# The last unit's outputs stored by quadrants instead of by whole rows

## The chip, the cores and the metric

The kernel runs on one core of a Trainium2 chip. The time is the device time of one execution in microseconds. Before the change, seven runs gave a median of 497.47 us, from 496.6 to 498.04.

## What is computed

A linear attention over 8 batches of 8 heads (576 positions, 64 features per head) feeds a mixture of 4 expert MLPs whose outputs are added with normalised weights:

```python
q_p, k_p = phi(q), phi(k)                       # elu + 1
kv = einsum('bhsd,bhse->bhde', k_p, v)
x = (q_p @ kv) / (q_p . sum(k_p))               # 4608 tokens x 512
p = probs / (probs.sum(-1) + 1e-9)
for e in range(4):
    h = maximum(x @ w1[e], 0)                   # 512 -> 1024
    out += p[:, e:e+1] * (h @ w2[e])            # 1024 -> 512
```

The output is 4608 x 512 in float32, 9.4 MB.

## The kernel before

**Tiles and units.** The 4608 tokens are cut into nine tiles of 512 tokens: tile j below 8 holds the first 512 positions of batch j; tile 8 holds the last 64 positions of all eight batches. One tile with one expert is a unit, and the units run tile by tile, the four experts within each; the last unit is (8, 3). A tile's output is four blocks of 128 tokens by 512 columns, `accs[j, ns]`, each an SBUF tile of 128 partitions with one row of 2 KB per token. In tile 8, block `ns` has the tokens of batch `2 * ns` in partitions 0 to 63 and of batch `2 * ns + 1` in 64 to 127.

**Layer 2 by seven products.** From tile 1 on, each 2 x 2 product of half matrices is done as seven products instead of eight (a Strassen scheme; the scheme's sums are made on VectorE and GpSimd). `layer2_product(j, e, ..., p, i)` does product `p` for token sub-block `i` (0 or 1): four matmuls of 128 x 256 into a PSUM tile, and then `add_acc` (L562), which scales it by the expert's weight and adds it to one *quadrant*: block `ns` and columns `ds`, either the left half `c1` or the right half `c2`. A table at L677 says which: product 2 and 1 go to the left half of block `i`, 6 and 3 to its right half, 5 and 7 to the right half of block `2 + i`, and 4 to its left half. The adds run on VectorE (L570). In the last unit the order of the products is 1, 2, 6, 5, 7, 3, 4 (L965), each for `i` = 0 and then 1, and two pairs of PSUM buffers, `pb` and `pe`, take turns.

**The stores.** After product 3 or 4 of expert 3 the block is complete, and `store` (L548) writes it out. For tiles 0 to 7 that is one DMA from the SP queue, 128 rows of 2 KB (L551). For tile 8 it is two DMAs, one for each half of the partitions, since those are two batches (L557): `u = 0` goes from SP's queue and, in the last tile, `u = 1` from ACT's. So the kernel ends with eight stores of 128 KB each: for `i` = 0 and 1 after product 3, and for `i` = 0 and 1 after product 4.

**Order.** The order of all the work is written out by hand: each step has a position (`put_at`), the list is sorted by position and issued in that order, and each engine keeps its own order. Which instruction waits for which is derived by the framework from the parts of tiles that they read and write. Each DMA from SP or ACT tells of its landing on one of eight semaphores, which are taken in turn. At the very end (L1020) the program waits until all DMAs have landed and then runs through a short barrier of all the engines.

Of the kernel before, what the change touches and what calls it, by code (L numbers as in the profile page):

```python
# [80 lines left out]
def kernel(  # L81
# [10 lines left out]
    nc = tc.nc  # L92
    ATTN, HSUM, L2ORD, L2AT, MODE = (CFG[x] for x in ("ATTN", "HSUM", "L2ORD", "L2AT", "MODE"))

    B, H, S, D = q.shape
    N, E = moe_domain_probs.shape
    _, Dm, F = moe_w1.shape
# [4 lines left out]
    SM = CM * P  # L102
# [7 lines left out]
    NTILES = N // NT  # L110
# [62 lines left out]
    out_b = out.rearrange("(b s) d -> b s d", s=S)  # L173
# [341 lines left out]
    accs = {}  # L515
# [29 lines left out]
    def new_py():  # L545
        return ppm.tile([P, Dm], FP32, tag="py", bufs=2, name="py")

    def store(j, ns, last=False):  # L548
        acc = accs[j, ns]
        if j < B:  # L550
            nc.sync.dma_start(  # L551
                out=out_b[j, 0:SM].rearrange("(p c) d -> c p d", c=CM)[ns],
                in_=acc,
            )
        else:
            for u in range(2):
                (nc.scalar if last and u else nc.sync).dma_start(  # L557
                    out=out_b[2 * ns + u, SM:S],
                    in_=acc[u * HP : (u + 1) * HP],
                )  # L560

    def add_acc(j, e, ns, ps, ds, first):  # L562
        if (j, ns) not in accs:
            accs[j, ns] = pm.tile([P, Dm], FP32, tag="acc", bufs=NACC, name="acc")
        acc = accs[j, ns][:, ds]
        pscal = p_sb[:, j, ns, e : e + 1]
        if first:
            nc.scalar.activation(acc, ps, AF.Identity, scale=pscal)
        else:
            nc.vector.scalar_tensor_tensor(  # L570
                out=acc, in0=ps, scalar=pscal, in1=acc, op0=AO.mult, op1=AO.add
            )

    def layer2_part(j, e, ns, hT, part, parts):
        if part == 0:
            pys[ns] = new_py()
        py = pys[ns]
        for fj in range(part * FC // parts, (part + 1) * FC // parts):
            nc.tensor.matmul(  # L579
                out=py,  # L580
                lhsT=rows(hT, fj)[:, ns * P : (ns + 1) * P],
                rhs=w2_sb[e][:, fj, :],
                start=(fj == 0),
                stop=(fj == FC - 1),
            )
        if part == parts - 1:
            add_acc(j, e, ns, py, slice(0, Dm), e == 0)
            if e == E - 1:
                store(j, ns)
# [53 lines left out]
    def layer2_product(j, e, hT, hss, p, i):  # L643


        if (j, e) == (NTILES - 1, E - 1):
            if p == 1:
                pys[i] = [ppm.tile([P, DH], FP32, tag=tag, bufs=2, name=f"p{tag}") for tag in ("b", "e")]
            run, side = pys[i]
        else:  # L650
            if p == 2:
                pys[i] = new_py()
            run, side = pys[i][:, 0:DH], pys[i][:, DH:Dm]
        ts = slice(i * P, (i + 1) * P)
        ts2 = slice(NH + i * P, NH + (i + 1) * P)
        w, tw = w2_sb[e], t2_sb[e]
        lo, hi = slice(0, FH), slice(FH, FC)
        ps, lhsT, rhs, first = {
            1: (run, lambda k: hT[k // 2][:, k % 2, 0, ts], w[:, lo, 0:DH], (j, e) == (NTILES - 1, E - 1)),
            2: (side, lambda k: hT[k // 2][:, k % 2, 1, ts], w[:, hi, 0:DH], True),  # L660
            5: (side, lambda k: hss[k // 2][0][:, k % 2, ts], tw[:, 0], True),
            6: (run, lambda k: hss[k // 2][1][:, k % 2, ts], tw[:, 1], False),
            7: (run, lambda k: hT[k // 2][:, k % 2, 0, ts2], w[:, lo, DH:Dm], False),
            3: (side, lambda k: hss[k // 2][3][:, k % 2, ts], w[:, hi, DH:Dm], False),
            4: (run, lambda k: hT[k // 2][:, k % 2, 1, ts2], tw[:, 2], False),
        }[p]
        for k in range(FH):
            nc.tensor.matmul(  # L668
                out=ps,
                lhsT=lhsT(k),  # L670
                rhs=rhs[:, k],
                start=first and k == 0,
                stop=k == FH - 1,
                skip_group_check=True,
            )
        c1, c2 = slice(0, DH), slice(DH, Dm)
        ns, ds, first = {  # L677
            2: (i, c1, True),
            5: (2 + i, c2, True),
            1: (i, c1, False),  # L680
            6: (i, c2, True),
            7: (2 + i, c2, False),
            3: (i, c2, False),
            4: (2 + i, c1, True),
        }[p]
        add_acc(j, e, ns, ps, ds, first and e == 0)
        if e == E - 1 and p in (3, 4):
            store(j, ns, j == NTILES - 1)

    tts = {}  # L690

# [171 lines left out]
    with tc.manual_schedule(  # L863
# [87 lines left out]
        for n, (j, e) in enumerate(units):  # L951
            h, hss = [None, None], [[None] * 4, [None] * 4]
            at = base + 2 * NSLOT * n
            for d in range(2):
                put_block(at + d * NSLOT, j, e, d, h)
            at += 2 * NSLOT + LAG

            def hsum(d, i, hT=h, hss=hss):
                hidden_sum(hT[d], hss[d], i)

            for d in range(2):
                for i in range(4):
                    put_at(at + HSUM[d][i], hsum, d, i)
            order = L2ORD
            if n == len(units) - 1:  # L965
                order, at = (1, 2, 6, 5, 7, 3, 4), at + NSLOT
            for m in range(14):
                put_at(at + L2AT[m], layer2_product, j, e, h, hss, order[m // 2], m % 2)
# [56 lines left out]
```

## Time and profile before

| What | Before |
|---|---|
| Median of 7 runs | 497.47 us (496.6 to 498.04) |
| The profiled execution's own time | 497.47 us |
| Its span, first to last instruction | 495.2 us |
| TensorE clock granted | 0.999 of full |
| Sub-block adds on L570, one add of 128 x 256 | 0.48 us, starting 0.44 us apart in the last unit |
| Stores of tiles 0 to 7 (L551): 256 KB, SP, to landing | 2.5 us (median of 32) |
| Stores of tile 8 on SP (L557): 128 KB, to landing | 2.7 us (median of 4) |
| Stores of tile 8 on ACT (L557): 128 KB, to landing | 3.3 us (median of 4) |

The profile is one execution. It lists, for each engine, what ran when and what it waited for. TensorE appears as PE (the products) and PEld (the loading of weights), VectorE as DVE, ScalarE as ACT, GpSimd as POOL and SyncE as SP; a "q" behind the name means the engine's instruction queue, where DMAs are issued and semaphores are waited for. A DMA has two durations: how long its issue occupies the queue (the duration in the timeline), and how long it is from the start of the issue until the data has landed.

### The profile page before, as it was taken

How to read it: one execution, taken by the hardware profiler on the slowest of the kernel's cores; microseconds unless marked ns; L12 is line 12 of the kernel's file. 1: busy time of each engine (PE TensorE's matmuls, PEld its weight loads, DVE VectorE, ACT ScalarE, POOL GpSimd, SP SyncE). 2: the span in 40 equal slices, each digit the busy share in tenths (PEclk: the TensorE clock that was granted, in tenths of full speed). 3: DMA queues.
4: the chain of work that ended last, by engine and by line, in shares of the span. 5: the costliest groups of instructions: out<-in, count | busy, mean ns of one | idle time of the engine just before them, and what ended most of it. 6: DMA issues, size and time to landing. Idle time of an engine off the chain costs nothing.

```text
span 495.2 us, 11600 instructions
## 1 busy us (share of the span) xinstructions
PE 483.5 (98%) x4346; PEld 409.5 (83%) x4346; DVE 378.7 (76%) x802; ACT 336.5 (68%) x678; POOL 354.7 (72%) x339
## 2 busy tenths in 40 slices
PE   8999989999999999999999999999999999999995
PEld 3556656888898989898989898989898888888884
DVE  5757888798867887698859886888687756775685
ACT  5776969964987498848884789468954565446530
POOL 3735204778967897769776977697769877987773
PEclk9999999999999999999999999999999999999999
DMA  8999965552455245533463245523141020002002
GB/s 258 211 220 240 272 137 161 175 117 52 112 175 129 54 109 171 126 64 96 144 155 78 76 145 139 101 63 104 68 79 28 5 95 1 1 3 85 1 1 86
DMA packets 81561, 53.65 MB, mean 108 GB/s; under 512 B 46113, under 2 KB 74785, under 8 KB 81505
## 3 DMA queue, kind: packets, MB, share of 16 engines
q1 hardware_dynamic: 70272, 40.07, 30.9%
q0 software_dynamic: 9824, 11.27, 12.1%
q10 hardware_dynamic: 1408, 1.57, 1.0%
q8 instruction: 34, 0.56, 0.5%
q14 instruction: 23, 0.18, 0.1%
HBM read 45.16 MB, written 9.44 MB: 110 GB/s over the span
## 4 chain that ended last, share of the span: by engine, by line
PE 82%; DMA 10%; DVE 3%; POOL 1%; ACT 1%; issue 1%; ACTq 0%; DVEq 0%; POOLq 0%
PE py L668 38%; PE pb L730 22%; PE pe L730 16%; DMA w<-in_moe_w_dram 7%; DMA rawu<-in_q_dram 2%; PE py L579 2%; PE psum_nd L465 1%; DMA rawh<-in_k_dram 1%; PE psum_kv L425 1%; DVE acc L570 1%; DVE x_sb L448 1%; PE pb L668 1%; DVE h L714 0%; PE psum_nl L482 0%; PE pe L668 0%
## 5 line engine op out<-in xcount | busy, mean ns | idle before, releaser
L570 DVE SCALAR_TENSOR_TENSOR acc<-py,p_sb,acc 128x256 f32<-128x256 f32 (+1 forms) x382 | 182.3, 488 | 49.3 <-PE py L668 40.1
L714 DVE CUSTOM_DVE_ANT_0 h<-pe,u 128x512 f16<-128x512 f32 x140 | 96.3, 688 | 41.8 <-PE pe L730 26.8
L730 PEld LDWEIGHTS <-w 128*128 128x128 f16 x1120 | 108.8, 98 | 17.0 <-issue 1.4
L635 POOL TENSOR_TENSOR hs<-h 128x512 f16<-128x512 f16 x64 | 74.0, 1156 | 54.9 <-DVE h L714 53.6
L668 PEld LDWEIGHTS <-h 128*128 128x128 f16 x1024 | 99.6, 98 | 11.8 <-issue 0.5
L668 PE MATMUL py<-w,h 128*128 128x256 f16 x744 | 106.4, 273 | 0.0
L741 ACT COPY u<-pb 128x512 f32<-128x512 f32 x140 | 82.8, 591 | 27.5 <-PE pb L730 25.1
L637 POOL TENSOR_TENSOR hs<-hs,h 128x512 f16<-128x512 f16 x64 | 74.7, 1168 | 26.7 <-PE py L668 24.1
L730 PEld LDWEIGHTS <-s 128*128 128x128 f16 x840 | 81.6, 98 | 11.8 <-DVE s L607 0.4
L730 PE MATMUL pb<-tt,w 128*128 128x256 f16 x560 | 84.0, 273 | 0.7 <-ACT u L741 0.7
L668 PEld LDWEIGHTS <-hs 128*128 128x128 f16 x768 | 74.4, 98 | 9.9 <-issue 1.3
L641 POOL TENSOR_TENSOR hs<-h,hs 128x512 f16<-128x512 f16 x64 | 74.7, 1166 | 3.5 <-PE py L668 3.1
L668 PE MATMUL py<-t,hs 128*128 128x256 f16 x496 | 74.4, 272 | 0.6 <-DVE acc L570 0.4
L639 POOL TENSOR_TENSOR h<-h 128x512 f16<-128x512 f16 x64 | 74.5, 1165 | 0.0
L756 ACT ACTIVATE h<-pe 128x512 f16<-128x512 f32 x70 | 41.9, 598 | 44.9 <-PE pe L730 44.4
L750 ACT COPY pe<-pb 128x512 f32<-128x512 f32 x70 | 40.3, 575 | 41.5 <-PE pb L730 14.9
L774 ACT ACTIVATE h<-pb 128x512 f16<-128x512 f32 x70 | 41.9, 599 | 9.8 <-PE pb L730 9.7
L730 PE MATMUL pb<-tt,s 128*128 128x256 f16 x280 | 42.0, 273 | 0.1
L730 PE MATMUL pe<-tt,s 128*128 128x256 f16 x280 | 42.0, 273 | 0.0
L730 PE MATMUL pb<-xT,w 128*128 128x256 f16 x248 | 37.2, 273 | 0.2
L730 PE MATMUL pe<-xT,s 128*128 128x256 f16 x248 | 37.2, 273 | 0.1
L668 PE MATMUL py<-w,hs 128*128 128x256 f16 x248 | 37.2, 273 | 0.0
(120 smaller groups left out, 605.7 us busy)
## 6 DMA issues: line engine op xcount, KB each, us to landing
out_dram<-acc SPq DMA_DIRECT2D x32, 256.0 KB, 2.5
w<-in_moe_w_dram POOLq DMA_DIRECT2D x14, 512.0 KB, 13.0
rawb<-in_v_dram SPq DMA_DIRECT2D x26, 256.0 KB, 2.8
rawb<-in_q_dram SPq DMA_DIRECT2D x26, 256.0 KB, 2.8
rawb<-in_k_dram SPq DMA_DIRECT2D x26, 256.0 KB, 3.2
w<-in_moe_w_dram POOLq DMA_DIRECT2D x4, 256.0 KB, 5.8
rawb<-in_k_dram POOLq DMA_DIRECT2D x4, 256.0 KB, 11.4
rl<-in_q_dram SPq DMA_DIRECT2D x16, 64.0 KB, 2.6
```

Source lines behind the costliest of these rows:

```text
L570: nc.vector.scalar_tensor_tensor(out=acc, in0=ps, scalar=pscal, in1=acc, op0=AO.mult, op1=AO.add)
L635: nc.gpsimd.tensor_tensor(out=hs[0], in0=a21, in1=a22, op=AO.add)
L637: nc.gpsimd.tensor_tensor(out=hs[1], in0=hs[0], in1=a11, op=AO.subtract)
L639: nc.gpsimd.tensor_tensor(out=a21, in0=a11, in1=a21, op=AO.subtract)
L641: nc.gpsimd.tensor_tensor(out=hs[3], in0=a12, in1=hs[1], op=AO.subtract)
L668: nc.tensor.matmul(out=ps, lhsT=lhsT(k), rhs=rhs[:, k], start=first and k == 0, stop=k == FH - 1, skip_group_check=True,)
L714: nc.vector._custom_dve(TENSOR_ADD_SAT, out=out, in0=ps, in1=u, s0=BIG, s1=0.0)
L730: nc.tensor.matmul(out=ps[:, kk], lhsT=lk(kc), rhs=rhs[:, kc], start=first and kk == 0 and kc == 0, stop=kc == 1, skip_group_check=True,)
L741: nc.scalar.copy(u, self.b)
L750: nc.scalar.copy(self.e5, self.b)
L756: nc.scalar.activation(self.h[:, :, 0, 0:NH], self.e5, AF.Relu)
L774: nc.scalar.activation(self.h[:, :, 1, 0:NH], self.b, AF.Relu)
```

## The change

For the last unit alone, a store is made as soon as a quadrant is complete instead of a block: after products 2, 7, 3 and 4, for both values of `i`, `store` is called with the columns `ds` of that product. Each such store is 64 partitions by 256 columns, rows of 1 KB to every second KB of the output: 64 KB, once from SP and once from ACT. For all other units the calls are as before. The argument `last` goes, since the branch with two DMAs serves tile 8 only.

```diff
-    def store(j, ns, last=False):
-        acc = accs[j, ns]
+    def store(j, ns, cols=slice(0, Dm)):
+        acc = accs[j, ns][:, cols]
         if j < B:
             nc.sync.dma_start(
                 out=out_b[j, 0:SM].rearrange("(p c) d -> c p d", c=CM)[ns],
...
             for u in range(2):
-                (nc.scalar if last and u else nc.sync).dma_start(
-                    out=out_b[2 * ns + u, SM:S],
+                (nc.scalar if u else nc.sync).dma_start(
+                    out=out_b[2 * ns + u, SM:S, cols],
                     in_=acc[u * HP : (u + 1) * HP],
                 )
...
         add_acc(j, e, ns, ps, ds, first and e == 0)
-        if e == E - 1 and p in (3, 4):
-            store(j, ns, j == NTILES - 1)
+        if (j, e) == (NTILES - 1, E - 1):
+            if p in (2, 3, 4, 7):
+                store(j, ns, ds)
+        elif e == E - 1 and p in (3, 4):
+            store(j, ns)
```

## The prediction

> **What bounds the kernel, and where the change acts.** I read the engine shares first, then the last microseconds as a timeline, then the stretches after the last product.
>
> ```profile
> PE 483.5 (98%) x4346; PEld 409.5 (83%) x4346; DVE 378.7 (76%) x802; ACT 336.5 (68%) x678; POOL 354.7 (72%) x339
> ```
>
> TensorE bounds the body, and the diff touches no product, so only what follows the last products can move. The timeline's columns are start, duration, engine and line:
>
> ```profile
> 484.65 0.92 DVE L570 SCALAR_TENSOR_TENSOR acc<-pe,p_sb,acc 128x256 f32<-128x256 f32 x2
> ...
> 487.27 0.92 DVE L570 SCALAR_TENSOR_TENSOR acc<-pb,p_sb,acc 128x256 f32<-128x256 f32 x2
> ...
> 488.14 0.92 DVE L570 SCALAR_TENSOR_TENSOR acc<-pe,p_sb,acc 128x256 f32<-128x256 f32 x2
> ...
> 488.66 2.48 SPq L557 DMA_DIRECT2D out_dram<-acc  x4
> 488.66 2.77 ACTq L557 DMA_DIRECT2D out_dram<-acc  x4
> 489.02 0.92 DVE L570 SCALAR_TENSOR_TENSOR acc<-pb,p_sb,acc 128x256 f32<-128x256 f32 x2
> ```
>
> These pairs of adds are products 2, 7, 3 and 4 of the last unit. The last add ends at 489.94, yet the span ends at 495.2: 5.2 us in which no engine computes. The view of stretches (PE, PEld, DVE, ACT, POOL busy; clock; DMA share; GB/s) says what fills them:
>
> ```profile
> 490.00:491.00 1.00, 0.00 (x0) 0.00 (x0) 0.00 (x0) 0.00 (x0) 0.00 (x0) 1.00 0.99 279
> 491.00:492.00 1.00, 0.00 (x0) 0.00 (x0) 0.00 (x0) 0.00 (x0) 0.00 (x0) 1.00 0.88 295
> 492.00:493.00 1.00, 0.00 (x0) 0.00 (x0) 0.00 (x0) 0.00 (x0) 0.00 (x0) 1.00 0.92 305
> 493.00:494.00 1.00, 0.00 (x0) 0.00 (x0) 0.00 (x0) 0.00 (x0) 0.00 (x0) 1.00 0.37 137
> ```
>
> The eight 128 KB stores, 1.05 MB, keep the DMA engines 90% busy: a burst at some 300 GB/s. Read singly, the landings are:
>
> SP issues 488.66, 489.30, 489.94, 490.58; landings 491.05, 491.73, 492.91, 493.89.
> ACT issues 488.66, 489.33, 490.17, 490.83; landings 491.39, 492.72, 493.54, 494.07.
>
> The first land after 2.39 (SP) and 2.73 us (ACT), the last after 3.31 and 3.24. From 494.07, the kernel's exit takes 1.10 us to the span's end at 495.17. So **the end is set by the landing of the last ACT store**. The profiled execution took 497.47 us, 2.3 more than its span, and is equal to the median; I sum against it.
>
> The last issues are themselves late: their add ends at 489.94, they start at 490.58 and 490.83. The rows of the two queues say why (min/median/max ns):
>
> ```profile
> L557 SPq DMA_DIRECT2D out_dram<-acc x4: 547/551/552, 488.7 to 490.6; - x4
> L557 ACTq DMA_DIRECT2D out_dram<-acc x4: 571/612/802, 488.7 to 490.8; - x4
> ```
>
> An issue occupies its queue for 0.55 to 0.61 us, from start to next start 0.64 on SP (1.92 / 3) and 0.72 on ACT (2.17 / 3), while adds come every 0.44.
>
> **Part 1: twice the stores, half the size.** Eight stores of 128 KB become sixteen of 64 KB: 64 partitions by 1 KB. In the order 1, 2, 6, 5, 7, 3, 4 the last product of each quadrant is indeed 2, 7, 3 or 4, so the change does what it says. Nothing is removed but bytes per store. Four pairs move ahead: those after product 2 (ready 485.13, 485.57) and after product 7 (ready 487.75, 488.19). SP and ACT have nothing else queued (ACT's last activation ends at 480.27), so nobody waits behind them except the later stores. That is the price: each queue gets six issues from 487.75 on, where it had four from 488.63.
>
> What does such an issue cost? No store of this form is in the trace. Two rows are near:
>
> ```profile
> L551 SPq DMA_DIRECT2D out_dram<-acc x32: 332/357/604, 80.7 to 448.7; - x32
> ...
> L253 SPq DMA_DIRECT2D rl<-in_q_dram x16: 597/614/639, 65.4 to 379.8; - x16
> ```
>
> The first is a store of 128 partitions with a strided destination, the second a 64 KB transfer over 64 partitions. Both 64-partition forms, L557 and L253, are the dear ones, so I take L557's pitch, 0.64 and 0.72, and keep 0.42 (0.33 + 0.09) and 0.84 (0.80 + 0.04) as ends.
>
> Starting at 487.78 (0.03 after the add, as at 488.66), with A and B for product 2's two stores on a queue, C and D for product 7's, G and H for product 4's:
> SP: C 487.78, D 488.42, then 489.06, 489.70, 490.34, H 490.98.
> ACT: C 487.78, D 488.50, then 489.22, 489.94, 490.66, H 491.38.
> So **H goes out 0.40 (SP) and 0.55 us (ACT) later than today**.
>
> **Part 2: the landing after H.** Per DMA engine, one store is four packets; 2 KB packets of this burst took 84 ns, 1 KB packets of the loads 46. A halved store saves 4 x 38 ns = 0.15 us; an ACT store behind its SP twin saves that twice. Unloaded landings become 2.39 - 0.15 = 2.24 and 2.73 - 0.30 = 2.43. They stay unloaded if the DMA engines keep up: a pair is 8 x 46 = 0.37 us of packets in each 0.64 to 0.72. Then SP's H lands at 493.22, ACT's at 491.38 + 2.43 = **493.81, 0.26 us before 494.07**. The burst's queueing goes (some 0.8 us of landing), and most of it is given back in issue time.
>
> [...]
>
> **Part 3: a new wait on the store's semaphore.** Loads and stores from SP and ACT rotate over eight semaphores, and an issue waits until its predecessor on the same one has landed. The start of the kernel shows it: the ninth transfer goes out at 3.72 when the first ACT load landed at 3.70, others at 4.85 for 4.83 and 6.43 for 6.41.
>
> ```profile
> 3.72 1.04 SPq L275 DMA_DIRECT2D rawb<-in_v_dram  x2
> 4.85 0.42 SPq L275 DMA_DIRECT2D rawb<-in_q_dram  x1
> 6.43 0.37 SPq L275 DMA_DIRECT2D rawb<-in_k_dram  x1
> ```
>
> Eight stores in the tail used each semaphore once; sixteen use it twice: product 3's stores wait for product 2's (long landed), G for C, H for D. D lands at 488.42 + 2.24 = 490.66 (SP) and 488.50 + 2.43 = 490.93 (ACT), 0.32 and 0.45 us before H's turn: hidden by the queue. If D's landing takes over 2.9 us, H waits.
>
> **Part 4: a wait of the adds on a store?** Product 6 adds to the right half of a block whose left half is being read by a store. If the whole tile were guarded, its add would wait. The nearest case is x_sb: the transpose issued at 365.91 reads one part and lands at 368.39, and VectorE writes another part at 367.00:
>
> ```profile
> 365.91 1.19 SPq L509 DMA_TRANSPOSE xT<-x_sb  x1
> ...
> 367.00 0.56 DVE L448 TENSOR_TENSOR x_sb<-psum_nd,recip 128x384 f16<-128x384 f32 x1
> ```
>
> So parts are guarded apart, and I cost this at nothing. The `last` argument's removal costs nothing: the else branch only serves the last tile.
>
> **Sum.** -0.26 us: 497.47 - 0.26 = **497.2**. With the ACT pitch at its usual 0.67 it is -0.5; with 0.84, +0.34.
>
> **The rivals.**
> 1. *Issue is cheap.* If a strided half row issues at 0.42, H is no longer queue-bound (487.78 + 2.10 = 489.88) but held by D: issued 488.22, landed on ACT 490.65. H lands at 493.08: -0.99, **496.5**; with landings nearer to the 2.07 of L551's quiet stores, 496. For: L551's 0.33 with a strided destination. Against: both 64-partition rows.
> 2. *Slower: the DMA side charges by the transfer, not the byte.* The burst served eight stores from first packet 489.86 to last 493.64: 0.47 each. If that is per transfer, twelve from 488.98 (C's issue + 1.20) end at 494.62, plus 0.43 to land: 495.05, +1.0, **498.5**, with H also held by a late D. It decides from 0.39 us per transfer, (494.07 - 0.43 - 488.98) / 12. For: the very first store's packets took 161 ns, not 84, and ACT's began only 0.61 us after them. Against: the next ones began 0.33 to 0.36 apart, which is the byte price 4 x 84.
> 3. *The adds wait for stores.* Product 6's add waits from 485.52 to A's landing, 485.16 + 2.43 = 487.59: +2.07. Then product 4's (491.09) waits for C's (487.78 + 2.07 + 2.43 = 492.28): +1.19. With the gain, +3.0: **500.5**. Only x_sb speaks against it, plainly.
>
> **How the numbers follow.** A measurement here tells no change from about 0.2%, 1.0 us: faster is below 496.5, slower above 498.5. The forecast gets 0.56 (its own range 496.6 to 498.0, from the pitches; 0.04 faster, 0.48 same, 0.04 slower); rival 1 gets 0.20 (0.15 faster, 0.05 same); rival 2 gets 0.19 (0.15 slower, 0.04 same); rival 3 with anything unforeseen 0.05, slower. Sums: 0.19, 0.57, 0.24. The range runs from rival 1 to just past rival 2, leaving out the tails of 1, 2 and 3: 496.3 to 498.7.
>
> **What would show it.** Right: issues on L557 still 0.55 to 0.6 us, back to back from 487.8; H starting near 491.0 and 491.4, landing after some 2.3; the stretch 490 to 493 at a DMA share near half. Wrong: issues of 0.35, H starting at D's landing, ACT landings over 3 us, or an idle gap on VectorE ahead of products 6 or 4.

## The result and the profile after

The changed kernel takes **496.07 us** (median of 15 runs, 495.25 to 497.33) against 497.45 before (35 runs): ratio 0.9973, 95% interval 0.9966 to 0.9980, or 1.0 to 1.7 us less. The forecast was 497.2, with no change as the likeliest case and a range from 496.3: too slow, and the measured time lies 0.23 us below the range. Two later series gave 0.9979 (0.9973 to 0.9986) and 0.9975 (0.9966 to 0.9983).

The rows of the store line in the changed kernel (count, min/median/max ns of an issue, first and last start):

```profile
L557 SPq DMA_DIRECT2D out_dram<-acc x8: 467/547/553, 484.3 to 490.0; - x8
L557 ACTq DMA_DIRECT2D out_dram<-acc x8: 498/557/856, 484.3 to 490.3; - x8
...
DMA to landing us min/median/max: 1.9/2.0/3.7
```

An issue costs what it did, 0.55 us, though its store is half as large; a landing takes 2.0 us where the last ones took 3.3. The stretches after the last add, which ends at 489.05 here (PE, PEld, DVE, ACT, POOL busy; clock; DMA share; GB/s):

```profile
488.00:489.00 1.00, 0.53 (x5) 0.22 (x3) 1.00 (x3) 0.00 (x0) 0.00 (x0) 1.00 0.85 196
489.00:490.00 1.00, 0.00 (x0) 0.00 (x0) 0.05 (x1) 0.00 (x0) 0.00 (x0) 1.00 0.89 204
490.00:491.00 1.00, 0.00 (x0) 0.00 (x0) 0.00 (x0) 0.00 (x0) 0.00 (x0) 1.00 0.88 203
491.00:492.00 1.00, 0.00 (x0) 0.00 (x0) 0.00 (x0) 0.00 (x0) 0.00 (x0) 1.00 0.82 185
492.00:493.50 1.50, 0.00 (x0) 0.00 (x0) 0.00 (x0) 0.00 (x0) 0.00 (x0) 0.95 0.02 5
```

The burst of 300 GB/s has become an even stream of 200, and it ends before 492, not after 493. The DMA engines are still 82 to 89% busy: the packets have become slower for their size, of which more below.

Two numbers of each profile carry the study: the **tail**, from the end of the last add to the last landing, and the **exit**, from there to the end of the span. Issue and landing of the last stores, counted from the last add's end:

| | SP's last issue, landing | ACT's last issue, landing | Tail | Exit |
|---|---|---|---|---|
| Before, first profile | +0.65, +3.96 | +0.89, +4.14 | 4.14 | 1.10 |
| Forecast | +1.04, +3.28 | +1.44, +3.87 | 3.87 | 1.10 |
| After | +0.97, +3.01 | +1.29, +3.32 | 3.32 | 1.09 |

The spans of this first pair differ by 1.71 us, but only 0.82 of that is tail. The last add itself comes 0.89 earlier, and all of that is won in the first 160 us (0.86 of it by 70), where the two kernels have the same instructions. It is the spread of single executions, and the experiments have to part it from the change.

### The profile page after: what moved, and what is told of

Its sections match the earlier page's. It is cut to its first block, busy times and chain, and to the rows that moved or that the text cites. A ratio compares the mean times of both kernels' runs of the same rounds, so it can differ in the third digit from the quotient of the medians.

```text
span 493.5 us, 11616 instructions
## 1 busy us (share of the span) xinstructions
PE 482.6 (98%) x4346; PEld 409.2 (83%) x4346; DVE 378.4 (77%) x802; ACT 336.4 (68%) x678; POOL 354.6 (72%) x339
## 4 chain that ended last, share of the span: by engine, by line
PE 84%; ACT 7%; DVE 4%; DMA 2%; issue 1%; POOL 1%; ACTq 0%; DVEq 0%; POOLq 0%
PE py L668 38%; PE pb L733 22%; PE pe L733 16%; PE py L579 2%; PE ph L524 1%; PE psum_nd L465 1%; DVE x_sb L448 1%; ACT psum_ee L315 1%; ACT u L744 1%; DMA rawh<-in_k_dram 1%; DVE acc L570 1%; PE psum_kv L425 1%; DMA rawb<-in_v_dram 1%; ACT h L759 1%; ACT vp L332 1%
## 5 line engine op out<-in xcount | busy, mean ns | idle before, releaser
L733 PE MATMUL pe<-xT,w 128*128 128x256 f16 x248 | 37.2, 272 | 0.0
```

The lines of the kernel that those rows point to most:

```text
L733: nc.tensor.matmul(out=ps[:, kk], lhsT=lk(kc), rhs=rhs[:, kc], start=first and kk == 0 and kc == 0, stop=kc == 1, skip_group_check=True,)
```

## The experiments

**Twice more the changed kernel, once more the one before.** No edit.

> The changed kernel once more, to part what is lasting from what varies. In the first pair of profiles the last add to the last landing took 4.13 us before and 3.32 after (0.81 less), while the last add itself came 0.89 us earlier, all of it gained in the first 64 us, where no instruction differs. Theory 'tail': only the 0.81 are the change's; the median comes out 0.7 to 1.0 below the kernel before and the tail again at 3.3. Theory 'more than the tail': the median is again 1.3 to 1.5 below, and the last add or the time outside the span is again earlier by some 0.5.

> The changed kernel a third time, beside the former on the same chip: 0.8 to 1.1 us faster than the kernel before, tail 3.3, and the last landing 1.1 before the end of the span.

> The kernel before once more, with a profile. In the first profile of it the execution's own time was 2.30 us more than its span, in all eight others so far 1.77 to 1.87, so 0.5 us of the change's gain lie outside the span. Theory 'lasting': again 2.3 outside the span, and a tail of 4.1. Theory 'spread of one execution': 1.8 outside. The time itself: no change against the kernel before.

The three profiles of the changed kernel have tails of 3.32, 3.30 and 3.30 us; the two of the kernel before 4.14 and 4.25. The last add came at 489.05, 489.78 and 490.18 after, at 489.94 and 490.15 before. The tail's gain of 0.9 us is thus lasting. The series: 0.9979 and 0.9975 for the changed kernel as above, 1.0002 (0.9995 to 1.0010) for the kernel before. In the first profile of before, the execution's time was 2.3 us over its span, here 1.84. All the series together say more than these two: of 170 executions of the kernel before, 36 took 2.2 to 2.4 us outside their span and the others 1.9 at most; of 152 of the changed kernel and its variants, none took more than 2.04. On average the kernel before thus loses 0.1 to 0.2 us there against the changed one. What causes it stays open.

**Instructions alone.** Does the changed kernel gain from the mere number of instructions on the queues?

```diff
+        if (j, e, p) == (NTILES - 1, E - 1, 2):
+            for m in range(4):
+                (nc.scalar if m % 2 else nc.sync).dma_start(
+                    out=extra[:, i, m : m + 1], in_=moe_domain_probs[m * P : (m + 1) * P, 0:1]
+                )
```

> The kernel before, with eight tiny loads (one float per partition, never read) added ahead of the last stores, four on SP's and four on ACT's queue: as many instructions more as the change brings, all landed long before the tail. Theory 'the time outside the span hangs on the count of instructions on a queue': 1.8 outside the span as in the changed kernel, the tail still 4.1, and 0.5 us faster than the kernel before. Theory 'it hangs on the stores' (or on nothing): 2.3 outside, no change in the time.

Ratio 1.0005 (0.9997 to 1.0014), tail 4.29, 1.78 us outside the span. None of its 13 executions took over 1.9 us there, but the 0.5 us of gain that the theory forecast lies outside the interval: instructions alone don't make the changed kernel's time.

**Half size, but not early.**

```diff
-            if p in (2, 3, 4, 7):
-                store(j, ns, ds)
+            if p in (3, 4):
+                store(j, ns, c1)
+                store(j, ns, c2)
```

> Both halves of a block are stored, but only when the block is complete (after products 3 and 4): stores of half the size, none of them early. Theory 'the queue': eight issues each on SP and ACT, 0.64 us apart, from 1.28 us before the last add's end; the last starts 3.2 after it and lands 2.05 later: tail 5.2 to 5.3, 1.1 us slower than the kernel before. Theory 'size': shorter stores land sooner and that was the gain: tail 3.3 to 3.9. Theory 'bytes left': as many bytes after the last products as before, so tail 4.1, no change.

Ratio 1.0012 (1.0005 to 1.0018), tail 4.86. The rows of the line:

```profile
L557 SPq DMA_DIRECT2D out_dram<-acc x8: 512/576/845, 485.5 to 493.1; - x8
L557 ACTq DMA_DIRECT2D out_dram<-acc x8: 483/589/619, 485.5 to 492.8; - x8
```

So small stores alone make the kernel slower. One thing in the edit differed from what I had written: the first block's left half needs product 2's add alone, and as nothing stood before it in the queues, its pair went out at -4.78 although it was written behind product 3. That leaves seven issues on each queue from -1.28; SP's last starts at +2.81, 0.68 us a step, and lands 2.05 later: 4.86. Each of the late stores lands in 2.0 to 2.3 us, as in the changed kernel; the wait is in the queue.

**All from one queue.**

```diff
-                (nc.scalar if u else nc.sync).dma_start(
+                nc.sync.dma_start(
```

> All sixteen quadrant stores are issued from SP. Theory 'the queue': twelve issues 0.64 us apart from product 7's add, which ends 2.19 before the last one; the last starts at -2.16 + 11 x 0.64 = 4.88 and lands 2.04 later: tail 6.9, 3.6 us slower than the changed kernel. Theory 'bytes left': the same bytes at the same times, tail 3.3, no change against the changed kernel. Theory 'semaphores': the wait for the store eight places earlier adds to the former only if that store takes over 5 us to land; no wait seen.

Ratio 1.0072 (1.0058 to 1.0086), tail 8.19. In the rows of the line:

```profile
L557 SPq DMA_DIRECT2D out_dram<-acc x16: 546/569/1968, 485.0 to 495.9; - x16
...
DMA to landing us min/median/max: 2.0/2.0/3.4
```

Sixteen issues follow each other from 485.0 to 495.9. My 6.9 fell short because SP was not free when product 7's stores came up: one of product 2's issues took 1.97 us. After that the step is 0.64, and every store lands 2.0 after its issue. That the same bytes are ready at the same times does nothing for the end; the queue sets it. The wait for the semaphore's former user never showed: eight steps of 0.64 are 5.1 us, over twice a landing.

**Relief from a third queue.**

```diff
-                (nc.scalar if u else nc.sync).dma_start(
+                (nc.gpsimd if pool else nc.scalar if u else nc.sync).dma_start(
...
-                store(j, ns, ds)
+                store(j, ns, ds, p == 7)
```

> Product 7's four stores are issued from GpSimd, which is idle then; SP and ACT have the rest. Theory 'the queue': on SP and ACT four issues are left after product 3's add, so the last starts 0.64 (SP) and 0.7 to 0.9 (ACT) after the last add instead of 0.97 and 1.29 and lands 2.05 later: tail 2.9, 0.4 us faster than the changed kernel, unless GpSimd's own four issues of 0.7 us and their landings end later still (then about equal). Theory 'bytes left': no change against the changed kernel, tail 3.3.

Ratio 0.9984 (0.9978 to 0.9991): no better than the changed kernel. The issues did what the queue theory said: SP's last at +0.56 and ACT's at +0.87. But they landed after 2.56 and 2.45 us, not 2.03, and the tail is 3.32 again (exit 1.35).

```profile
489.00:490.00 1.00, 0.27 (x3) 0.00 (x0) 0.79 (x2) 0.00 (x0) 1.00 (x3) 1.00 0.66 132
490.00:491.00 1.00, 0.00 (x0) 0.00 (x0) 0.00 (x0) 0.00 (x0) 0.07 (x1) 1.00 0.87 258
491.00:492.00 1.00, 0.00 (x0) 0.00 (x0) 0.00 (x0) 0.00 (x0) 0.00 (x0) 1.00 0.97 270
```

The DMA share rises to 0.97 at 270 GB/s, and the last four stores land 0.20 us apart (+2.71, +2.91, +3.12, +3.32). The wait has moved from the queues to the DMA engines. Both limits lie close together.

**One half of the change at a time.** Products 2 and 3 split, the other blocks whole; then products 7 and 4 split.

```diff
-            if p in (2, 3, 4, 7):
+            if p in (2, 3):
                 store(j, ns, ds)
+            elif p == 4:
+                store(j, ns)
```

The second edit is the same with `(7, 4)` for the halves and `3` for the whole blocks.

> Only the first two blocks are stored by halves (after products 2 and 3); the other two go out whole after product 4, so nothing is issued after product 7. Theory 'the queue and the last landing': four issues from product 3's add, the last 0.65 (SP) and 0.9 (ACT) after the last add, of 128 KB, landing 2.4 to 2.7 later: tail 3.3 to 3.6, that is 0.6 to 0.8 faster than the kernel before. Theory 'bytes moved early': half the bytes of the change are moved ahead, so half its gain: tail 3.7.

> Only the last two blocks are stored by halves (after products 7 and 4); the first two go out whole after product 3. Theory 'the queue and the last landing': six issues from product 7's add as in the changed kernel, the last 0.97 and 1.3 after the last add, of 64 KB, landing 2.05 to 2.3 later: tail 3.3 to 3.6. Theory 'bytes moved early': half the gain, tail 3.7. If the first two kinds are both near 3.3, either half of the change is worth nearly all of it.

The first: ratio 0.9991 (0.9984 to 0.9997), tail 3.35, exit 1.34; last issues at +0.57 and +0.86, landings 2.41 and 2.48 later. The second: 0.9990 (0.9982 to 0.9999), tail 3.68, exit 1.35; last issues at +1.07 and +1.38, landings 2.40 and 2.31. Neither theory takes both: the first has nearly the whole tail gain with a queue as short as before, and the second, with the changed kernel's long queue and its small last stores, sits 0.08 past the queue theory's range and at the value of "bytes moved early". In it the last landings are 0.3 to 0.4 longer than 2.03; the whole rows of product 3 land only up to +2.83, after the last issues. So it isn't the size of the last store alone: what the DMA engines still hold when it arrives counts too.

**One issue per quadrant.** If the queue costs 1 us at the end, one issue in place of two should take it back. The two batches of a block lie in the output 64 rows each, so a single store over 128 partitions needs tile 8's tokens in another order: the two batches taking turns.

```diff
-            for u in range(2):
-                (nc.scalar if u else nc.sync).dma_start(
-                    out=out_b[2 * ns + u, SM:S, cols],
-                    in_=acc[u * HP : (u + 1) * HP],
-                )
+            turn["st"] = turn["st"][::-1]
+            turn["st"][0].dma_start(
+                out=out_b[2 * ns : 2 * ns + 2, SM:S, cols].rearrange("u r d -> r u d"),
+                in_=acc,
+            )
...
-        return bts[j].xT if j < B else xT_left
+        return bts[j].xT if j < B else mixed[0]
+
+    def mix_left(dc):
...
+        nc.scalar.copy(
+            out=mixed[0][:, dc].rearrange("p (b r u) -> p b u r", u=2, r=HP),
+            in_=xT_left[:, dc].rearrange("p (b u r) -> p b u r", u=2, r=HP),
+        )
...
```

> The tokens of tile 8 are put in another order (the two batches of a block take turns row by row), so that a quadrant is one store over 128 partitions with one issue, SP and ACT in turn; for that ScalarE makes four copies of the leftover inputs during tile 7, and the probabilities are loaded in the same order. Theory 'the queue': one issue per add, and the queue is always free; the last starts 0.03 after the last add and lands 1.7 to 2.1 later (the 256 KB stores of 128 partitions land 2.07 after their issue): tail 1.7 to 2.2, 1.1 to 1.6 us faster than the changed kernel, some 2.2 faster than the kernel before. Theory 'bytes': the same bytes at the same rate of some 200 GB/s end no sooner: tail 3.3. Theory 'the copies cost': up to 2.4 us of ScalarE in tile 7 come onto the path, and the last add is later by that.

> The same order of tile 8's tokens, but the blocks stored whole (256 KB each, one issue, after products 3 and 4). The last issue starts 0.03 after the last add as well. Theory 'the queue alone': the tail is that of the quadrant version plus the longer packets of one store, 0.4 us: 2.2 to 2.6. Theory 'bytes left count once the queue is free': four stores of 0.83 us of packets start 0.85 after the first issue at -1.28, so they end at 2.9 and land at 3.3: tail 3.3, about 1.3 slower than quadrants.

> The quadrants over 128 partitions again, with ScalarE's four copies two to three slots later: in the first version the copy at 411.70 put off two scalings and TensorE lost 0.57 us there, the three others lost nothing. Theory 'the queue': tail 2.1 as before, and the last add no later than in the changed kernel but for the spread of the start: 2.0 to 2.2 us faster than the kernel before, 1.1 to 1.3 faster than the changed kernel. Theory 'the copies cost wherever they are': again some 0.6 is lost, 1.5 faster than the kernel before.

With quadrants: ratio 0.9966 (0.9953 to 0.9979), tail 2.11, the last issue at +0.03. With whole blocks: 0.9995 (0.9987 to 1.0004), tail 3.26, though its last issue starts at +0.03 too: here the bytes decide, and storing by quadrants is worth 1.15 us of tail. In both, TensorE lost 0.57 us at the first copy:

```profile
412.86 0.60 PE L677 MATMUL py<-w,h 128*128 128x256 f16 x4 [0.42 <-ACT acc L577]
```

With the copies two to three slots later (positions 38, 40, 42, 45 for 36 to 42) that is gone: **494.96 us, ratio 0.9955** (0.9942 to 0.9968), against 496.11 and 0.9975 for the changed kernel on the same chip. It beats both kernels: its six runs took 494.78 to 495.69 us, the changed kernel's twelve 495.66 to 496.75. Its rows and stretches:

```profile
L566 SPq DMA_DIRECT2D out_dram<-acc x4: 538/560/651, 485.1 to 489.5; - x4
L566 ACTq DMA_DIRECT2D out_dram<-acc x4: 546/547/654, 485.5 to 489.9; - x4
```

```profile
489.00:490.00 1.00, 0.35 (x4) 0.07 (x1) 0.87 (x2) 0.00 (x0) 0.00 (x0) 1.00 0.96 319
490.00:491.00 1.00, 0.00 (x0) 0.00 (x0) 0.00 (x0) 0.00 (x0) 0.00 (x0) 1.00 0.93 309
491.00:492.00 1.00, 0.00 (x0) 0.00 (x0) 0.00 (x0) 0.00 (x0) 0.00 (x0) 1.00 0.46 152
```

An issue costs 0.55 here too, so the 64 partitions are not what makes an issue dear; what makes those of tiles 0 to 7 cheap (0.33 to 0.36) stays open. And the stream runs at 319 GB/s where the changed kernel's ran at 200.

**Do tail and exit account for the times?** Before, they add up to 5.24 and 5.35, mean 5.29 us. Each kernel's sum less 5.29, with the 0.57 for the two that lost it, over 497.3:

| Kernel | Tail + exit | Ratio from it | Ratio measured |
|---|---|---|---|
| changed | 4.41, 4.39, 4.39 | 0.9982 | 0.9973, 0.9979, 0.9975 |
| before, instructions alone | 5.49 | 1.0004 | 1.0005 |
| half size, late | 5.90 | 1.0012 | 1.0012 |
| all from SP | 9.22 | 1.0079 | 1.0072 |
| product 7 from GpSimd | 4.67 | 0.9988 | 0.9984 |
| split 2 and 3 | 4.69 | 0.9988 | 0.9991 |
| split 7 and 4 | 5.03 | 0.9995 | 0.9990 |
| 128 partitions, quadrants | 3.03 + 0.57 | 0.9966 | 0.9966 |
| 128 partitions, whole | 4.43 + 0.57 | 0.9994 | 0.9995 |
| 128 partitions, copies moved | 3.04 | 0.9955 | 0.9955 |

All but one lie within the measured intervals; the first series of the changed kernel misses by 0.0002. For that kernel the sum gives 0.9 us and the three series 1.0 to 1.3. In the second series the difference closes: its mean span is 0.87 us shorter than that of the kernel before, and the mean time outside the span 0.19. In the third the span is 1.20 shorter and the time outside it 0.12, so some 0.3 us stays open; for the first the record has no spans of the kernel before, and 0.4 stays open. The last add shows no lasting shift that could be told from its spread.

## Why the prediction was wrong

- **What bounds the kernel** was right: the gain that the profiles show is in the tail, and the exit is the same (1.10 and 1.09).
- **Issue cost and pitch on SP** were right: 0.547 us and 0.64 a step; the last SP issue came at +0.97, forecast +1.04. Rival 1, cheap issue for strided rows, fell: even 128 partitions cost 0.55.
- **The pitch on ACT** was taken as 0.72 from three gaps, one of which had a long issue (802 ns). In a row of six only one was long (856 ns): the last issue came at +1.29, not +1.44. That is 0.15 us of the error.
- **The step that failed is the landing of the halved store** in part 2, and in it the wait of ACT's store behind its SP twin. The landing was to be 2.24 us on SP and 2.43 on ACT; measured were 2.04 and 2.03. ACT's 0.40 and the pitch's 0.15 make up the 0.55 between the tails of 3.87 and 3.32.

  *ACT, which sets the end.* In the kernel before, ACT's first store had its first packet 1.81 us after its issue, SP's twin after 1.21: a wait of 0.6 us. I took off 0.15 of it. In the changed kernel the last ACT store has its first packet after 1.21, so all of the wait is gone, and I was 0.46 short. Its own packets gave 0.09 (0.55 to 0.46 us), 0.06 less than my 0.15; that leaves the 0.40. The two queues are 0.32 us out of step since ACT's one long issue, so the last stores no longer meet. Where they still are in step, at the first pair after product 7, ACT has its first packet after 1.42 and lands 0.28 us after SP (2.23 against 1.95); there 0.3 us of the wait is left. So halving took some 0.3 of the 0.6, and being out of step the rest. My account didn't have them out of step; the long issue came in all three profiles of the changed kernel (850 to 856 ns), and why it is long stays open.

  *SP.* I priced the halving by the burst's packets, 84 ns for 2 KB and 46 for 1 KB, at 0.15 us. But the 2.39 that I started from was the landing of SP's first store of before, which ran almost alone, and its packets were slower. It ran from 489.86 to 490.70, 0.84 us, with packets of 161 ns (median); the last SP store of after ran from 491.22 to 491.67, 0.45 us, with packets of 76. The views of the DMA queues, before from 489.8 to 490.5 and after from 491.2 to 491.7 (packets, MB, share of the 16 engines' time):

```profile
q1 hardware_dynamic: 63, 0.13, 89.0%
```

```profile
q1 hardware_dynamic: 80, 0.07, 58.1%
```

  In the first, 0.89 of 16 x 0.7 us over 63 packets is 158 ns each. In the second, 16 of the 80 packets have only 4 bytes and take 9 ns each; that leaves a mean of 70 ns. Halving saved 0.4 us of packets and 0.36 of SP's landing, not 0.15. The 161 ns stood in my text, but only as an argument for rival 2.
- **What this step does not explain.** With the measured tail the sum would have been 497.47 - 0.82 = 496.65, inside my range. The rest down to 496.07, some 0.6 us, is not in the tail of the profiles. In the two repeated series this rest was 0.2 and 0.4, of which 0.1 to 0.2 was time outside the span; for the first series its cause stays open.
- **DMA share "near half"** was wrong because of the slower packets: 0.82 to 0.89, with 1 KB packets of some 75 ns. In the experiments the 1 KB packets of stores over 128 partitions took 46 ns, so the figure that I had used was right for those.
- **The semaphores** (part 3) were right: the last SP issue at +0.97 found its predecessor landed at +0.43, ACT's at +1.29 one of +0.71.
- **The adds don't wait for stores** (part 4): product 2's store of block 0 was issued at 484.28 and landed at 487.74, and product 6's add to the other half of that block started at 484.64, on the usual step of 0.44 us. Rival 3 fell.

```profile
484.28 0.55 SPq L557 DMA_DIRECT2D out_dram<-acc  x1
484.28 0.57 ACTq L557 DMA_DIRECT2D out_dram<-acc  x1
484.64 0.48 DVE L570 SCALAR_TENSOR_TENSOR acc<-pb,p_sb,acc 128x256 f32<-128x256 f32 x1
```

- **Rival 1** had named 496.5, nearer to the measured time than my 497.2. That is no merit of its mechanism: the issues stayed at 0.55 us.
- **Rival 2**, a price per transfer, fell: twelve stores from product 7 on came 0.32 us apart in the even stream, under its break-even of 0.39. Its mechanism was half real: the slow packets were there, but they shrink with the row.
- **Issue time** (part 1) belonged in the sum. Late halves (a step of 0.68 us, tail 4.86) and the single queue (0.64, tail 8.19) show that it is no small thing next to a landing of 2.0 us.

## What to carry to other kernels

At the end of a kernel, count three things: when the last issue can leave its queue, what the DMA engines still hold then, and the bare landing (2.0 us for the stores here). In this kernel, splitting the stores helped only as far as it emptied the second without filling the first: the same halves cost 0.6 us when late and saved 0.9 when early, and one issue per 128 partitions saved another 1.2 us of tail. Price a smaller transfer by the transfer of the same shape that ran alone, not by packets of a mixed burst (here 161 ns against 84), and ask whether it will still stand behind another one.

## What the hardware showed unexpectedly

- A store of 64 partitions by 1 KB, running mostly alone, had packets of 74 to 76 ns (median; some 0.45 us in all); one of 128 partitions by 1 KB had 46 ns (0.53 us in all), so twice the bytes took little longer. For 2 KB packets it was 161 ns over 64 partitions and 85 over 128. Where stores of both partition halves stood in the DMA engines together, 64 partitions had the fast packets too: 84 ns for 2 KB in the burst of before, 46 for 1 KB in the last stores of the GpSimd run and of the second half change. No run here shows the cause.
- The early stores of product 2 landed only after 3.3 to 3.7 us. While they ran, one 16 KB instruction fetch took 0.95 us, from 485.74; all but 14 of the 256 packets of 1 KB of those stores were done by 486.92, and these 14 ran one after another until 487.73. The view of DMA queues from 484 to 488 of the changed kernel shows the fetch as

```profile
q8 instruction: 1, 0.02, 1.5%
```

  That the fetch is what they waited for fits the times but was not tried. In four profiles (the second of the changed kernel, the single queue, the GpSimd run and the first half change) the fetch fell into one of product 2's issues. That issue took 1.75 to 2.06 us and ended 0.4 us after the fetch in each; it is the long one that delayed the single queue. Here too only the times speak.
- The exit goes with the semaphore that the last landing uses: the closing waits take the eight one after the other, some 0.06 us each. The last landing was on the fifth in the changed kernel (exit 1.09), on the first in the two half changes and the GpSimd one (1.34 to 1.35), and on the last in the quadrants over 128 partitions (0.92 and 0.93). The run with instructions alone had 1.20 on the fifth; there the closing barrier took 0.1 us more.
- Single executions of one kernel differ by up to 2 to 3 us within a series, and the profiles place the differences between them in the first 160 us; after that, but for the 0.57 us named above, the traces run alike to 0.03 us until the tail.
